# A decode attention kernel: K and V loaded in units of eight heads through a ring of three unequal regions

## The chip, the core and the metric

The kernel runs on one core of one Trainium2 chip. The metric is device time in microseconds (us) of one execution. The engines that appear below are TensorE (PE, with its weight loads shown apart as PEld), VectorE (DVE), ScalarE (ACT), GpSimd (POOL) and SyncE (SP), which issues nearly all transfers. On-chip memory is SBUF, with 128 partitions, and PSUM, which TensorE accumulates into in eight banks of 512 float32 columns per partition.

## What is computed

Two rows of `x` (batch 2, one token, 512 wide, bf16) go through two branches that a gate mixes. Cut to what matters, the reference is:

```python
g = sigmoid((x * gate_w).sum(-1, keepdims=True))
q = (x @ wq).reshape(2, 1, 32, 128)                     # 32 heads of 128
scores = einsum("bhqd,bhkd->bhqk", q, k_cache) * 128**-0.5    # k_cache: 2 x 32 x 4096 x 128
p = softmax(scores)
a = einsum("bhqk,bhkd->bhqd", p, v_cache).reshape(2, 1, 4096) @ wo
b = relu(x @ w1) @ w2                                   # 512 -> 1376 -> 512
out = g * a + (1 - g) * b
```

`k_cache` and `v_cache` are 64 MiB each; `wq` and `wo` are 4 MiB each, `w1` and `w2` 1.4 MB each. Everything is bf16. Each byte of K and V is used once.

## The kernel before

**Units and slots.** K is cut into 16 units of 4 MiB (four heads each), V likewise. Unit `u` holds 16,384 consecutive rows of 128 values, laid out so that partition `p` takes 128 consecutive rows: 32 KB per partition, one contiguous run in memory. The tile `kv` has `NSLOT` = 3 slots of 32 KB per partition; K units 0 to 15 and then V units 0 to 15 go through the slots in turn (`order`, `slot_of`, lines 188 to 199). `wreg` (32 KB per partition) is a separate tile that holds `wq`, later `w1`, later `wo`; `w2` has a tile of its own.

**Transfers.** They are all on SP's queue, in this order (lines 260 to 274): `wq`, K0 to K15, `w1` (it waits for `pe_q`, the end of the query projection, which frees `wreg`), V0 to V15, the last 96 rows of `w2`, two halves of `wo` (the first waits for `pe_h`, the end of `x @ w1`), three parts of `w2`, and the output. From the fourth unit on each transfer waits until its slot has been read: K units are read by the last of their four transposes (`kt_…`), V units by the last of their matmuls (`pe_v_…`). SP issues in order, so a transfer that waits holds back those behind it.

**K stage.** `k_turn` (line 379) is a VectorE transpose of a quarter of a unit into one of three buffers `kt` (`NKT` = 3); it sees pairs of bf16 as float32 and transposes blocks of 32 by 32. `k_scores` (lines 385 to 409) then does eight matmuls of 512 columns per turn: two weight loads, each held for four matmuls, one per PSUM bank. The weights are the queries, put into a buffer `qbuf` of zeros in such a way that a window of 128 columns places the result of each turn in its own rows of PSUM. All 64 turns accumulate in the same four banks. ScalarE copies the second batch's queries into `qbuf` as its parts come free (`q_second`).

**Softmax and spread.** `softmax` (lines 413 to 430) takes the maximum over all four banks (2,048 columns), brings it to one value per unit by two small transposes, lets ScalarE do four exponentials of 512 columns, and transposes the result back (line 427). `sm_spread` then copies the probabilities into `ptm`, block-diagonal weights whose zeros were set at the start; GpSimd, ScalarE and VectorE share this for the first group of four units, and GpSimd does the later groups.

**V stage.** `v_unit` (line 456) does 32 matmuls per unit with 16 weight columns each, four at a time on four column tiles of the array, into one PSUM bank. `v_extract` masks that bank and sums it into `X2` (lines 464 and 467); the next unit's matmuls wait for this. `x @ w1` (`ffn_h`, line 359) and its ReLU run on TensorE and VectorE after V1, the softmax denominators before V2.

**End.** `o_gather` sums `X2` into the heads' outputs, normalises and turns them into weights `oW`. `project` (line 498) multiplies them with `wo` in 32 matmuls: the first 16 wait for one half of `wo`, the others for the second. `ffn_f` (line 505) multiplies with `w2`, row group by row group, each part waiting for its own transfer, and adds the projection in between; `store` copies the result out of PSUM and the output transfer waits for both copying engines.

Order on every engine is the order in which the program lists its operations; waits are semaphores that each engine counts up.

Of the kernel before, what the change touches and what calls it, by code (L numbers as in the profile page):

```python
# [10 lines left out]
DFF = 1376  # L11
INV_SQRT_DH = 1.0 / (DH ** 0.5)

NSLOT = 3
NKT = 3

# [69 lines left out]
def bass_gated_mix__gqa_block_cached__dense_activation_relu__decode_kernel(  # L86
# [30 lines left out]
    kv = sb("kv", [128, NSLOT, 16384], dt.bfloat16)  # L117
    xTw = sb("xTw", [128, 4, 32], dt.bfloat16)
    qrow = sb("qrow", [128, 2, 4, 128], dt.bfloat16)
    wreg = sb("wreg", [128, 16384], dt.bfloat16)  # L120
    w2 = sb("w2", [128, 11, 512], dt.bfloat16)
    kt = sb("kt", [128, NKT, 2048], dt.float32)
    kt16 = kt[:, :, :].rearrange("p k n -> p (k n)").bitcast(dt.bfloat16).rearrange(
        "p (k c n two) -> p k c n two", k=NKT, c=4, two=2)
    qbuf = sb("qbuf", [128, 8, 4, 160], dt.bfloat16)
    E_sb = kt[:, 0, :].bitcast(dt.bfloat16)[:, 0:2048].rearrange("p (c n) -> p c n", c=4)
    ET_sb = kt[:, 0, :].bitcast(dt.bfloat16)[:, 2048:4096].rearrange("p (c n) -> p c n", c=4)
    ptm = sb("ptm", [128, 2, 16, 4, 2, 4, 4], dt.bfloat16)
    mpad = sb("mpad", [128, 32], dt.float32)
    mrow = sb("mrow", [128, 32], dt.float32)  # L130
    mmax = sb("mmax", [128, 16], dt.float32)
    nrow = sb("nrow", [128, 16, 2], dt.float32)
    negm = sb("negm", [128, 32], dt.float32)
    lsum = sb("lsum", [128, 4], dt.float32)
    pr_sb = sb("pr_sb", [128, 512], dt.float32)
    sel2 = sb("sel2", [128, 2], dt.float32)
    lrow = sb("lrow", [128, 1], dt.float32)
    rinv = sb("rinv", [32, 2], dt.float32)
    mask3 = sb("mask3", [128, 8, 4, 4], dt.float32)
    maskc = sb("maskc", [128, 4], dt.float32)  # L140
    selx = sb("selx", [128, 60], dt.float32)
    sell = sb("sell", [128, 2, 8, 4], dt.float32)
    s4 = sb("s4", [32, 4, 128], dt.bfloat16)
    X2 = sb("X2", [128, 2, 8, 128], dt.float32)
# [14 lines left out]
    V_B = 6  # L159
# [14 lines left out]
    names = ["x", "gw", "wq", "w1", "wo0", "wo1", "w2a", "w2b", "w2c", "w2d", "out"]  # L174
    sem = {n: nc.alloc_semaphore("sem_" + n) for n in names}
    sem_slot = [nc.alloc_semaphore(f"sem_slot{s}") for s in range(NSLOT)]
# [11 lines left out]
    order = [("k", u) for u in range(16)] + [("v", u) for u in range(16)]  # L188
    place = {what: n for n, what in enumerate(order)}

    def slot_of(what):
        return place[what] % NSLOT

    def slot_wait(what):
        return (sem_slot[slot_of(what)], 16 * (place[what] // NSLOT + 1))

    def freed(what):
        kind, u = what
        return marker(f"kt_{4 * u + 3}") if kind == "k" else marker(f"pe_v_{u}")
# [11 lines left out]
    def pe(fn, waits=(), signal=None, dwaits=()):  # L211
# [10 lines left out]
    pool(lambda g: g.memset(mask3[:], 0.0), signal="c_m3z")  # L222
    pool(lambda g: g.affine_select(out=mask3[:].rearrange("p (t f) h c -> p t f h c", t=4)[:, :, 0],
                                   in_=mask3[:].rearrange("p (t f) h c -> p t f h c", t=4)[:, :, 0],
                                   pattern=[[-32, 4], [-4, 4], [-1, 4]],
                                   compare_op=ALU.not_equal, fill=1.0, base=0, channel_multiplier=1),
         waits=["c_m3z"], signal="c_m3")
    pool(lambda g: g.memset(sell[:], 1.0), signal="c_s1")
    pool(lambda g: g.affine_select(out=sell[:], in_=sell[:], pattern=[[-16, 2], [-2, 8], [-32, 4]],
                                   compare_op=ALU.is_ge, fill=0.0, base=0, channel_multiplier=1),  # L230
         waits=["c_s1"], signal="c_s2")
    pool(lambda g: g.affine_select(out=sell[:], in_=sell[:], pattern=[[16, 2], [2, 8], [32, 4]],
                                   compare_op=ALU.is_ge, fill=0.0, base=1, channel_multiplier=-1),
         waits=["c_s2"], signal="c_sell")
    pool(lambda g: g.memset(s4[:], 0.0), signal="c_s4z")
# [4 lines left out]
    pool(lambda g: g.memset(ptm[:], 0.0), signal="c_ptm")  # L240
# [9 lines left out]
    def unit_in(what):  # L250
        kind, u = what
        rows = k_rows if kind == "k" else v_rows
        return rows[u * 16384:(u + 1) * 16384, :].rearrange("(p r) d -> p (r d)", p=128)
# [7 lines left out]
    for n, what in enumerate(order):  # L261
        waits = [freed(order[n - NSLOT])] if n >= NSLOT else []
        sp(lambda e, what=what: e.dma_start(kv[:, slot_of(what), :], unit_in(what)).then_inc(sem_slot[slot_of(what)], 16),  # L263
           waits=waits)
        if n == 15:
            sp(lambda e: e.dma_start(wreg[:, 0:5504], w1_in).then_inc(sem["w1"], 16), waits=[marker("pe_q")])
    sp(lambda e: e.dma_start(w2[0:96, 10, :], B_w2[1280:1376, :]).then_inc(sem["w2a"], 16))
    sp(lambda e: e.dma_start(wreg[:, 0:8192], wo_in[:, 0:8192]).then_inc(sem["wo0"], 16), waits=[marker("pe_h")])
    sp(lambda e: e.dma_start(wreg[:, 8192:16384], wo_in[:, 8192:16384]).then_inc(sem["wo1"], 16))
    for name, r0, r1 in (("w2b", 0, 4), ("w2c", 4, 9), ("w2d", 9, 10)):  # L270
        sp(lambda e, name=name, r0=r0, r1=r1: e.dma_start(w2[:, r0:r1, :], w2a_in[:, r0:r1, :]).then_inc(sem[name], 16))
    sp(lambda e: e.dma_start(out.rearrange("b s n -> (b s) n"), out_sb[:, :]).then_inc(sem["out"], 16),
       waits=[marker("dve_out"), marker("act_out")])
# [3 lines left out]
    def gate():  # L277
        for t in range(4):
# [19 lines left out]
        dve(lambda v: v.tensor_reduce(out=maskc[:], in_=mask3[:].rearrange("p k h c -> p c (k h)"), axis=AX.X, op=ALU.add),  # L298
            waits=["c_m3"], signal="dve_maskc")
        dve(lambda v: v.tensor_reduce(out=mrow[:, :].rearrange("p (k h) -> p k h", h=4), in_=mask3[:], axis=AX.X, op=ALU.add),  # L300
            waits=["c_m3"], signal="dve_selx0")
        dve(lambda v: v.tensor_reduce(out=selx[:, 28:32], in_=mrow[:, :].rearrange("p (k h) -> p h k", h=4), axis=AX.X, op=ALU.add),
            waits=["dve_selx0", "c_selx"], signal="dve_selx")
        dve(lambda v: v.tensor_reduce(out=sel2[:], in_=ident16[:].rearrange("p (t q) -> p q t", t=4)[:, 0:2, :], axis=AX.X, op=ALU.add),
            waits=["c_i16"], signal="dve_sel2")
        dve(lambda v: v.memset(psf(0, 128, V_B * BANK, BANK), 0.0), signal="dve_v0")

    def q_window(b, hq, u0, u1):
        halves = qT_ps.rearrange("p (s j q m) -> p s q j m", s=2, j=4, q=4)
        if u1 - u0 == 8:  # L310
            out = qbuf[32 * hq:32 * hq + 32, :, :, 32 + 32 * hq].rearrange("p (s q) j -> p s q j", s=2)
            return out, halves[32 * hq:32 * hq + 32, :, :, :, b]
        return qbuf[32 * hq:32 * hq + 32, u0, :, 32 + 32 * hq], halves[32 * hq:32 * hq + 32, u0 // 4, u0 % 4, :, b]

    def q_proj():
# [25 lines left out]
        for hq in range(4):  # L341
            out, src = q_window(0, hq, 0, 8)
            act(lambda a, out=out, src=src: a.activation(out=out, in_=src, func=ACT.Copy),
                waits=["pe_q", "c_qbuf"], signal=f"q_0_{hq}")

    def q_second(uh):
        for hq in range(4):
            out, src = q_window(1, hq, uh, uh + 1)
            act(lambda a, out=out, src=src: a.activation(out=out, in_=src, func=ACT.Copy),  # L349
                waits=[f"pe_sc_{4 * uh + 3}"], signal=f"q_1_{uh}_{hq}")  # L350

    def ffn_h():
        for ft in range(11):
            m = 128 if ft < 10 else 96
            for t in range(4):
                def fn(e, ft=ft, t=t, m=m):
                    o = t * DFF
                    cols = wreg[:, o + ft:o + 1280:10] if ft < 10 else wreg[:, o + 1280:o + 1376]
                    return e.matmul(psf(0, m, H_C0 + 2 * ft, 2), lhsT=cols, rhs=xT3[:, t, 0:2], start=(t == 0), stop=(t == 3))  # L359
                pe(fn, dwaits=([(sem["w1"], 16)] if ft == 0 and t == 0 else []),  # L360
                   signal=("pe_h" if ft == 10 and t == 3 else None))
# [11 lines left out]
    def k_turn(i):  # L373
        u, k = divmod(i, 4)
        rr, h = divmod(k, 2)
        what = ("k", u)
        pairs = kv[:, slot_of(what), :].bitcast(dt.float32).rearrange("p (r h d) -> p h r d", h=2, d=32)
        dst = kt[:, i % NKT, :].rearrange("p (r n) -> p r n", n=32)
        dve(lambda v: v.transpose(out=dst, in_=pairs[:, h, 64 * rr:64 * rr + 64, :]),  # L379
            waits=([f"pe_sc_{i - NKT}"] if i >= NKT else []), dwaits=([slot_wait(what)] if k == 0 else []), signal=f"kt_{i}")  # L380
# [8 lines left out]
    def k_scores(i):  # L389
        u, k = divmod(i, 4)  # L390
        rr, h = divmod(k, 2)
        pos = 2 * u + rr
        for two in range(2):
            for c in range(4):
                first, last = two == 0 and c == 0, two == 1 and c == 3
                waits = [f"kt_{i}"] if first else []
                if first and k == 0:
                    waits += [f"q_1_{u - 8}_{hq}" if u >= 8 else f"q_0_{hq}" for hq in range(4)]

                def fn(e, two=two, c=c):  # L400
                    out = psf(0, 128, c * BANK, 512)
                    lhsT = qbuf[:, u % 8, 2 * h + two, 32 - pos:160 - pos]
                    rhs = kt16[:, i % NKT, c, :, two]
                    start, stop = i == 0 and two == 0, i == 63 and two == 1
                    if c == 0:
                        return e.matmul(out, lhsT=lhsT, rhs=rhs, start=start, stop=stop)  # L406
                    return mm_held(e, out, lhsT, rhs, start, stop)
                pe(fn, waits=waits, signal=(f"pe_sc_{i}" if last else None))
# [178 lines left out]
```

## Time and profile before

| | us |
|---|---|
| Time, median of 3 runs (lowest to highest) | 345.83 (345.66 to 346.14) |
| The profiled execution's own time | 345.78 |
| Its span, first to last instruction | 344.5 |
| DMA rate over the span | 423 GB/s, 145.57 MB |
| VectorE busy / TensorE busy in the span | 189.6 / 201.8 |
| First transpose of K0 / of K15 starts | 22.71 / 169.97 |
| First matmul on V0 / on V15 starts | 190.09 / 329.12 |
| Last matmul ends | 342.68 |

The busy shares are averages over stages with different limits, so they are read stage by stage. The profiled execution lies 1.3 us above its span, which is time outside the instructions, and 0.05 us below the median of the runs. A view of waits says what an engine waited for; the chain of waits follows back from the last instruction to what released it.

### The profile page before, as it was taken

How to read it: one execution, taken by the hardware profiler on the slowest of the kernel's cores; microseconds unless marked ns; L12 is line 12 of the kernel's file. 1: busy time of each engine (PE TensorE's matmuls, PEld its weight loads, DVE VectorE, ACT ScalarE, POOL GpSimd, SP SyncE). 2: the span in 40 equal slices, each digit the busy share in tenths (PEclk: the TensorE clock that was granted, in tenths of full speed). 3: DMA queues.
4: the chain of work that ended last, by engine and by line, in shares of the span. 5: the costliest groups of instructions: out<-in, count | busy, mean ns of one | idle time of the engine just before them, and what ended most of it. 6: DMA issues, size and time to landing. Idle time of an engine off the chain costs nothing.

```text
span 344.5 us, 2426 instructions
## 1 busy us (share of the span) xinstructions
PE 201.8 (59%) x1240; PEld 40.6 (12%) x856; DVE 189.6 (55%) x136; ACT 15.2 (4%) x51; POOL 25.7 (7%) x32
## 2 busy tenths in 40 slices
PE   0429877878788787878790774223446443223365
PEld 0200000000000000000000241000113111000132
DVE  0848998999998999999978221111112101111121
ACT  1040000000000000000004000000000000000000
POOL 8400000000000000000001500400040000000000
PEclk9999998999999999999997565665556866555678
DMA  8999999999999999999999999999999999999995
GB/s 324 434 453 434 426 424 426 426 426 437 437 445 436 419 434 426 430 426 430 448 425 434 430 424 430 426 430 426 439 437 434 424 441 430 430 426 430 417 407 219
DMA packets 5747, 145.57 MB, mean 423 GB/s; under 512 B 645, under 2 KB 874, under 8 KB 1130
## 3 DMA queue, kind: packets, MB, share of 16 engines
q1 hardware_dynamic: 5732, 145.43, 98.5%
q8 instruction: 8, 0.13, 0.2%
q14 instruction: 1, 0.01, 0.0%
q10 hardware_dynamic: 6, 0.00, 0.0%
HBM read 145.43 MB, written 0.00 MB: 422 GB/s over the span
## 4 chain that ended last, share of the span: by engine, by line
DMA 72%; DVE 18%; PE 7%; issue 1%; SPq 1%; ACT 0%; DVEq 0%
DMA kv<-in_A_k_cache_dram 35%; DMA kv<-in_A_v_cache_dram 27%; DVE kt L379 16%; DMA wreg<-in_A_wo_dram 10%; PE PS L456 5%; PE PS L385 1%; DVE mpad L414 1%; DVE kt L427 1%; DVE ptm L440 1%; PE PS L498 1%; PE PS L406 0%; SPq L263 0%; PE PS L505 0%; DVE pr_sb L501 0%; DVE out_sb L524 0%
## 5 line engine op out<-in xcount | busy, mean ns | idle before, releaser
L379 DVE STREAM_TRANSPOSE kt<-kv 128x2048 f32<-128x2048 f32 x64 | 142.2, 2280 | 18.6 <-DMA kv<-in_A_k_cache_dram 16.6
L385 PE MATMUL PS<-kt,qbuf 128*128 128x512 bf16 x384 | 109.4, 393 | 0.0
L456 PE MATMUL PS<-kv,ptm 128*16 128x512 bf16 x512 | 56.3, 619 | 89.0 <-DMA kv<-in_A_v_cache_dram 76.7
L464 DVE TENSOR_TENSOR pr_sb<-PS,maskc 128x512 f32<-128x512 f32 x16 | 11.1, 691 | 108.6 <-PE PS L456 108.6
L406 PE MATMUL PS<-kt,qbuf 128*128 128x512 bf16 x128 | 51.1, 399 | 32.3 <-DVE kt L379 32.3
L456 PEld LDWEIGHTS PS<-kv,ptm 128*16 128x16 bf16 x512 | 16.9, 124 | 127.7 <-issue 109.3
L442 POOL COPY ptm<-kt 32x512 bf16<-32x512 bf16 x13 | 14.4, 1113 | 232.0 <-DVE lrow L428 175.2
L406 PEld LDWEIGHTS PS<-kt,qbuf 128*128 128x128 bf16 x128 | 12.5, 98 | 147.2 <-DVE kt L379 106.4
L467 DVE TENSOR_REDUCE X<-pr_sb 128x128 f32<-128x512 f32 x16 | 16.3, 1021 | 0.5
L349 ACT ACTIVATE qbuf<-PS 32x4 bf16<-32x4 bf16 x32 | 5.7, 179 | 76.5 <-PE PS L385 75.9
L527 ACT ACTIVATE out_sb<-PS 2x128 bf16<-2x128 f32 x2 | 0.5, 271 | 153.9 <-PE PS L505 153.9
L424 ACT ACTIVATE kt<-PS,negm 128x512 bf16<-128x512 f32 x4 | 2.7, 686 | 80.4 <-DVE negm L421 80.4
L279 PE MATMUL PS<-ident,x_sb 3*128 3x3 bf16 x4 | 0.3, 166 | 8.0 <-DMA x_sb<-in_gate_w_dram 8.0
L282 DVE COPY xT<-PS 128x12 bf16<-128x12 bf16 x1 | 0.2, 170 | 8.3 <-PE PS L279 8.3
L498 PE MATMUL PS<-wreg,oW 128*2 128x512 bf16 x32 | 2.9, 499 | 2.6 <-DMA wreg<-in_A_wo_dram 1.7
L220 POOL MEMSET qbuf<- 128x5120 bf16 x1 | 4.4, 4370 | 0.0
L479 PE MATMUL PS<-X,selx 128*32 128x128 f32 x32 | 4.0, 273 | 0.3 <-DVE X L467 0.3
L284 DVE COPY xTw<-xT 128x8 bf16<-128x8 bf16 x1 | 4.1, 4085 | 0.0
L365 DVE TENSOR_SCALAR hT<-PS,gm 128x10 bf16<-128x10 f32 x2 | 0.5, 228 | 6.2 <-PE PS L359 6.2
L318 PE MATMUL PS<-wreg,xTw 128*32 128x512 bf16 x32 | 3.6, 628 | 0.0
L285 DVE TENSOR_TENSOR xg<-xT 128x8 f32<-128x8 bf16 x1 | 3.6, 3630 | 0.0
L479 PEld LDWEIGHTS PS<-X,selx 128*32 128x32 f32 x32 | 3.4, 110 | 1.3 <-DVE X L467 0.6
(66 smaller groups left out, 45.8 us busy)
## 6 DMA issues: line engine op xcount, KB each, us to landing
kv<-in_A_k_cache_dram SPq DMA_DIRECT2D x16, 4096.0 KB, 20.3
kv<-in_A_v_cache_dram SPq DMA_DIRECT2D x16, 4096.0 KB, 25.4
wreg<-in_A_wq_dram SPq DMA_DIRECT2D x1, 4096.0 KB, 12.2
wreg<-in_A_wo_dram SPq DMA_DIRECT2D x2, 2048.0 KB, 32.2
wreg<-in_B_w_dram SPq DMA_DIRECT2D x1, 1376.0 KB, 23.1
w<-in_B_w_dram SPq DMA_DIRECT2D x1, 640.0 KB, 36.4
w<-in_B_w_dram SPq DMA_DIRECT2D x1, 512.0 KB, 35.3
w<-in_B_w_dram SPq DMA_DIRECT2D x1, 128.0 KB, 36.2
```

The source lines that it names most:

```text
L220: pool(lambda g: g.memset(qbuf[:], 0.0), signal="c_qbuf")
L284: dve(lambda v: v.tensor_copy(out=xTw[:, :, 0:2], in_=xT), waits=["dve_xT", "c_xTw"], signal="dve_xTw")
L349: act(lambda a, out=out, src=src: a.activation(out=out, in_=src, func=ACT.Copy), waits=[f"pe_sc_{4 * uh + 3}"], signal=f"q_1_{uh}_{hq}")
L379: dve(lambda v: v.transpose(out=dst, in_=pairs[:, h, 64 * rr:64 * rr + 64, :]), waits=([f"pe_sc_{i - NKT}"] if i >= NKT else []), dwaits=( ...
L385: return e.add_instruction(mybir.InstMatmult(start_tensor_calc=start, stop_tensor_calc=stop, tile_size=(128, 128), tile_position=(0, 0), l ...
L406: return e.matmul(out, lhsT=lhsT, rhs=rhs, start=start, stop=stop)
L442: pool(lambda e, dst=dst, src=src: e.tensor_copy(out=dst, in_=src), waits=waits, signal=f"pt{g}_{hq}")
L456: pe(lambda e, n=n, t=t, a=a, r16=r16, grp=grp, u4=u4, rows=rows: e.matmul(psf(32 * t, 32 * t + 16, V_B * BANK, 512), lhsT=ptm[:, grp % 2, ...
L464: dve(lambda e: e.tensor_tensor(out=parts, in0=psf(0, 128, V_B * BANK, 512).rearrange("p (c d) -> p c d", c=4), in1=maskc[:].unsqueeze(2). ...
L467: dve(lambda e: e.tensor_reduce(out=X2[:, b, u8, :], in_=parts.rearrange("p c d -> p d c"), axis=AX.X, op=ALU.add), waits=[f"dve_m{v}"], s ...
L479: pe(lambda e, u=u, b=b: e.matmul(psf(0, 32, O_C0, 128), lhsT=selx[:, 28 - 4 * u:60 - 4 * u], rhs=X2[:, b, u, :], start=(u == 0), stop=(u ...
L498: pe(lambda e, r=r, t=t: e.matmul(psf(32 * t, 32 * t + 2, PR_C0, 512), lhsT=oW[:, r, :], rhs=wreg[:, r * 512:(r + 1) * 512], start=(r < 4) ...
```

## The change

K and V are now cut into eight units each, of eight heads and 8 MiB: 64 KB per partition, again one contiguous run. `kv` becomes one tile of five pieces of 32 KB (`HALF` elements each) with three regions in it: A and B of 64 KB, C of 32 KB. A unit is loaded whole into A or B, or in two halves at different times (`lo` and `hi`, each the first or second 32 KB of every partition's run). Of each cache six units go whole and two in halves, so there are ten transfers for K and ten for V where there were 16 and 16. `wq` is loaded into C, `w1` into the first part of B, and at the end `wo` into C and `w2` into the upper half of B; the tiles `wreg` and `w2` are gone as tiles of their own. `w1` is loaded directly behind `wq`, ahead of K, and `ffn_h` and `ffn_relu` move ahead of the K stage. Each transfer waits for the last reader of what its region held before.

A unit has eight turns instead of four. A turn's columns now fall into two parities (`par`), because the blocks of 16 positions alternate between two heads; `k_scores` has four weight loads per turn, each held for two matmuls. The softmax has two maxima per row, one for each parity. Four exponentials remain; two transposes of twice the size follow. The spread into `ptm` is now a VectorE multiplication of the probabilities with a mask (`mask8`), once per piece, into places that rotate; no zeroing of `ptm`. V's weights have 32 columns instead of 16, a whole unit has 64 matmuls, and pieces alternate between two PSUM banks. `ptm`, `X2` and `pr_sb` lie over `kt` and `qbuf`. `wo` is cut at row group 24 instead of 16. The copies of the result count up a semaphore of their own that the output transfer waits for.

```diff
-NSLOT = 3
+HALF = 16384
+REGION = {"A": 0, "B": 2 * HALF, "C": 4 * HALF}
+WO_CUT = 24
...
-    order = [("k", u) for u in range(16)] + [("v", u) for u in range(16)]
...
+    both, lo, hi = (0, 1), (0,), (1,)
+    k_pieces = [(0, both, "A"), (1, both, "B"), (2, lo, "C"), (3, both, "A"), (4, both, "B"), (2, hi, "C"),
+                (5, both, "A"), (6, both, "B"), (7, lo, "C"), (7, hi, "A")]
+    v_pieces = [(0, both, "B"), (1, lo, "C"), (2, both, "A"), (3, both, "B"), (1, hi, "C"), (4, both, "A"),
+                (5, both, "B"), (6, lo, "C"), (7, both, "A"), (6, hi, "B")]
...
+    holder, filled = {"A": None, "B": "pe_h", "C": "pe_q"}, {"A": 0, "B": 0, "C": 0}
+    for kind, n, u, halves, region in pieces:
+        predecessor[kind, n] = holder[region]
+        filled[region] += 1
+        landed[kind, n] = (sem_region[region], 16 * filled[region])
+        holder[region] = f"{kind}_read_{n}"
...
+    def piece_in(kind, u, halves):
+        runs = (k_rows if kind == "k" else v_rows)[u * 32768:(u + 1) * 32768, :].rearrange("(p r) d -> p (r d)", p=128)
+        return runs[:, HALF * halves[0]:HALF * (halves[-1] + 1)]
...
     sp(lambda e: e.dma_start(wreg[:, :], wq_in).then_inc(sem["wq"], 16))
+    sp(lambda e: e.dma_start(w1, w1_in).then_inc(sem["w1"], 16))
+    for kind, n, u, halves, region in pieces:
+        sp(lambda e, kind=kind, u=u, halves=halves, region=region:
+           e.dma_start(piece_sb(halves, region), piece_in(kind, u, halves)).then_inc(sem_region[region], 16),
+           waits=([marker(predecessor[kind, n])] if predecessor[kind, n] else []))
+    sp(lambda e: e.dma_start(w2[0:96, 10, :], B_w2[1280:1376, :]).then_inc(sem["w2a"], 16), waits=[marker("v_read_6")])
+    sp(lambda e: e.dma_start(wreg[:, 0:512 * WO_CUT], wo_in[:, 0:512 * WO_CUT]).then_inc(sem["wo0"], 16), waits=[marker("v_read_7")])
+    sp(lambda e: e.dma_start(wreg[:, 512 * WO_CUT:HALF], wo_in[:, 512 * WO_CUT:HALF]).then_inc(sem["wo1"], 16))
...
     def k_scores(i):
...
+        for par in range(2):
+            for two in range(2):
+                for g in range(2):
...
+                        lhsT = qbuf[:, u % 4, par, 2 * h + two, 32 - pos:160 - pos]
+                        rhs = kt16[:, i % NKT, g, :, par, :, two]
...
+    def v_spread(n, n0, n1):
...
+        dve(lambda v: v.tensor_tensor(out=v_weights(n)[:, n0:n1], in0=src.unsqueeze(2).to_broadcast([128, n1 - n0, 8, 4]),
+                                      in1=mask8[:].unsqueeze(1).unsqueeze(3).to_broadcast([128, n1 - n0, 8, 4]), op=ALU.mult),
+            waits=["dve_et1", "c_mask8"] + [f"v_read_{m}" for m in prev], signal=f"pt{n}_{n0}")
...
     gate()
     q_proj()
+    ffn_h()
+    ffn_relu()
     for i in range(64):
         k_turn(i)
         if i >= 1:
             k_scores(i - 1)
     k_scores(63)
     softmax()
-    for v in range(16):
...
+    v_spread(1, 0, 32)
+    for n in range(10):
+        if n + 2 < 10:
+            v_spread(n + 2, 0, 32 * len(v_pieces[n + 2][1]))
+        v_unit(n)
+        if n == 1:
             o_denominators()
+        v_extract(n)
+        if n == 5:
             o_gather(0)
     o_gather(1)
     project()
```

## The prediction

> **What bounds the kernel now.** I read the page's slices and DMA queues first, then VectorE's timeline through the K stage, then the chain of waits at its end.
>
> ```profile
> span 344.5 us, 2426 instructions
> ...
> DMA  8999999999999999999999999999999999999995
> ...
> DMA packets 5747, 145.57 MB, mean 423 GB/s; under 512 B 645, under 2 KB 874, under 8 KB 1130
> ...
> q1 hardware_dynamic: 5732, 145.43, 98.5%
> ```
>
> SP's queue (q1) keeps all 16 DMA engines busy for 98.5% of the span: the transfers are the bound, from the first slice to the last but one. The same bytes move in both kernels, so only four things can change the time: the cost per packet, a moment when the queue is empty, the rate, and the tail behind the last transfers.
>
> ```profile
> 22.71 8.89 DVE L379 STREAM_TRANSPOSE kt<-kv 128x2048 f32<-128x2048 f32 x4 [4.72 <-DMA kv<-in_A_k_cache_dram]
> 32.49 8.89 DVE L379 STREAM_TRANSPOSE kt<-kv 128x2048 f32<-128x2048 f32 x4 [0.88 <-DMA kv<-in_A_k_cache_dram]
> 42.21 8.89 DVE L379 STREAM_TRANSPOSE kt<-kv 128x2048 f32<-128x2048 f32 x4 [0.84 <-DMA kv<-in_A_k_cache_dram]
> 53.15 8.89 DVE L379 STREAM_TRANSPOSE kt<-kv 128x2048 f32<-128x2048 f32 x4 [2.05 <-PE PS L385]
> 62.87 8.89 DVE L379 STREAM_TRANSPOSE kt<-kv 128x2048 f32<-128x2048 f32 x4 [0.83 <-DMA kv<-in_A_k_cache_dram]
> ...
> 160.25 8.89 DVE L379 STREAM_TRANSPOSE kt<-kv 128x2048 f32<-128x2048 f32 x4 [0.82 <-DMA kv<-in_A_k_cache_dram]
> 169.97 8.89 DVE L379 STREAM_TRANSPOSE kt<-kv 128x2048 f32<-128x2048 f32 x4 [0.82 <-DMA kv<-in_A_k_cache_dram]
> ```
>
> A unit lands every 9.72 us and its four transposes take 8.89: VectorE follows the transfers with 0.82 us to spare per unit. (The 2.05 us before 53.15 is put down to PE, but PE's turn 9 had long ended; K3 landed late. An instruction fetch of 16 KB on queue 8 began at 48.6 us, and one DMA engine was 1.2 us behind the others from then on.)
>
> ```profile
> 304.54 34.47 DMA wreg<-in_A_wo_dram
> 339.00 0.04 issue
> 339.05 1.90 PE PS L498 x15
> 340.95 0.02 issue
> 340.97 0.70 DVE pr_sb L501
> 341.68 0.04 issue
> 341.72 0.96 PE PS L505 x32
> ```
>
> At the end the second half of `wo` lands at 339.00, and 3.7 us of compute follow it. The last packet of `w2` ended at 341.76 in the trace's packet records, so here the computing is last, by 0.9 us.
>
> **The change, part by part.**
>
> *Packets.* The packet records (no view prints single ones) have medians of 1,214 ns for 32,768 bytes (4,224 packets: K, V, `wq`), 615 for 16,384 (`wo`), 418 for 11,008 (`w1`), 200 for 5,120, 46 for 1,024, and 9 for the 4-byte packet that counts the semaphore. They lie on one line: 15 ns plus 0.0366 ns per byte. Eight packets per engine and the semaphore give 8 x 1.214 + 0.009 = 9.72 us, the landing step above: there is no gap between queued transfers. If a row of 64 KB is one packet it should take 15 + 2,397 = 2,412 ns where two took 2,428. A whole piece saves 8 x 16 + 9 = 137 ns, and 12 whole pieces save 1.64 us. The other end, if each row goes as two packets, is the 12 semaphore packets alone: 0.11 us. A loss is not excluded, since no row here is longer than 32 KB (rival D). I take 1.64, because five sizes over a factor of 32 lie on the line.
>
> The Trainium skill, page "DMA: Bandwidth & Descriptors", section "Anatomy of one DMA", gives each transfer a fixed cost of about 2.0 us. By it 12 fewer transfers would save an estimated 24 us; the 9.72 us step leaves no room for that, and the trace decides.
>
> *Does the queue run empty?* I replay the transfers with steps of 19.31 us per whole piece, 9.72 per half and 3.35 for `w1` (8 x 0.418 + 0.009). `wq` lands at 12.98 as before (K0 at 22.69 was two steps after the start), `w1` at 16.3, K0 at 35.6, K1 at 54.9, K2's first half at 64.7, K3 at 84.0, K4 103.3, K2's second half 113.0, K5 132.3, K6 151.6, K7's halves 161.3 and 171.0. Eight transposes take 7 x 2.207 + 2.27 = 17.72 us (the x4 row is 3 x 2.207 + 2.27), so VectorE reads K0 to 53.4, K1 to 72.8, K2 first half to 81.7, K3 to 101.8, K4 to 121.1, K2 second half to 130.0, K5 to 150.1, K6 to 169.4, K7 to 187.2. The new waits on SP, each with everything behind it on hold: K1 for `pe_h`, about 23 (K0's transfer covers it to 35.6); K3 for K0's read, 53.4 against 64.7, when the queue would be empty; K4 72.8 against 84.0; K5 101.8 against 113.0; K6 121.1 against 132.3; the K7 halves 130.0 and 150.1 against 151.6 and 161.3. Then V0 goes into B and waits for K6's read: 169.4 against 171.0. This is the one tight place. The first transfer's packets began 1.0 us after its issue (0.81 to 1.81), and the semaphore is seen 0.36 us after its packet. On the engine that sets the landings: 0.36 + 0.1 to the first transpose + 17.72 + 0.02 + 1.0 = 19.2 us after K6's last packet, and K7's halves last 19.44. So it stays fed by 0.2 us. The other engines had run up to 1.7 us ahead (the semaphore's first to last count is 1.7 to 1.9 us apart from 53 us on) and would lose that lead, and a cold first packet takes 1.9 us instead of 1.2. The cost lies between 0 and 1.2 us, the second if a later instruction fetch again makes a new engine the last by what it cost at 48.6. I take 0.3, as the engine that counts has its next packet in time.
>
> *Softmax and V.* The softmax starts at 187.2 + 2.0 for PE's last turn, against 180.9 before. Maximum 2.3, four small steps 0.9, exponentials and transposes 3.4, then half of V0's spread: no row has it; 1,024 elements at L464's rate (512 in 0.69) are 1.4 us, and a quarter to three times that changes nothing. V0's matmuls run from about 197 to 205 (64 where 32 took 3.6 us). V0's reader frees B for V3, whose turn on the queue comes at 219: 14 us of cover. Later pieces have more: each takes 3.6 or 7.2 us, and in the page PE idles 76.7 us waiting for V. The spreads (up to 2.8 us each on VectorE), 32 weight columns for 16 and two banks lie in that idle time. GpSimd loses its 3.5 us of zeroing and its copies, which nothing at the end waited for.
>
> *K scores.* Four weight loads per turn instead of two.
>
> ```profile
> 174.52 0.10 PEld L406 LDWEIGHTS PS<-kt,qbuf 128*128 128x128 bf16 x1 [1.40 <-DVE kt L379]
> 174.53 0.40 PE L406 MATMUL PS<-kt,qbuf 128*128 128x512 bf16 x1 [0.22 <-DVE kt L379]
> 174.76 0.84 PE L385 MATMUL PS<-kt,qbuf 128*128 128x512 bf16 x3
> 175.22 0.10 PEld L406 LDWEIGHTS PS<-kt,qbuf 128*128 128x128 bf16 x1 [0.60 <-issue]
> 175.44 0.39 PE L406 MATMUL PS<-kt,qbuf 128*128 128x512 bf16 x1
> ```
>
> From 174.53 to 175.44 four matmuls take 0.91 us, and the next load (0.10) lies beside them. Eight take 1.82; with two more loads wholly exposed 2.02, still under VectorE's 2.21. Cost nothing, with that cover. Waits between whole pieces grow to about 1.8 us, and PE ran one turn at half speed (3.4 us) after an idle 2.38; the three `kt` buffers hold back VectorE only beyond 4.4 us.
>
> *Moved work.* `w1` is as long on the queue at 13 us as at 170. Its 44 matmuls (2.7 us) and the four ReLU steps now run before K0 lands at 35.6, on engines that wait; likewise the eight query copies for four.
>
> *Tail.* Only eight matmuls follow the last part of `wo` instead of 16: 0.95 of the 1.90 us. The first part lands 2.4 us later (7.6 after V's last piece, where the weights `oW` are ready at 7.2: 329.1 to 336.3), and its 24 matmuls end between 9.1 and 10.4, with the last part landing at 10.1. Then `w2` is next: its last packet at 341.76 and four matmuls allow PE to end at about 342.1 instead of 342.68. Bounds 0 and 0.66 us; I take 0.5.
>
> *Sum.* -1.64 + 0.3 - 0.5 = -1.84 us on the profiled execution's 345.78: 343.9. It stands 0.05 us below the median, which I leave out.
>
> **Rivals.**
>
> *B, rows of 64 KB save nothing.* 345.78 - 0.11 + 0.3 - 0.5 = 345.5. For it: packets grow from 615 to 1,214, nearly by their bytes, so little is left to save.
>
> *C, the K stage gets a pace of its own (slower).* If a turn takes p us, V0's first packet comes at 35.7 + 56p + 1.0 once p is above 2.41 (19.31/8). The queue is empty from 171.0, so the gap reaches the 2.5 us that make the total 0.7 slower at p = 2.45; at p = 2.6 it is 11 us: about 355. For it: the matmuls now read their columns in runs of 16, and PE at half clock needs 3.4 us. Against it: 1.82 now, and half clock lasted one turn (55.5 to 58.9).
>
> *D, longer rows read more slowly (slower).* Partitions are 64 KB apart in memory instead of 32, also for halves. From B's 345.5 a loss of 0.43% on the 233 us of whole pieces is enough for slower; 1% gives 347.8. Against it: `w1`'s rows 11 KB apart and `wo`'s and K's 32 KB apart lie on one line.
>
> On the same page of the Trainium skill, "Latency and other measured facts" has copies slowed by wide power-of-two row pitch, 207 GB/s against 214 at 512 KiB. An estimate by that 3.3% on K and V would be some 10 us more, and no run here has shown such a pitch.
>
> **How the numbers follow.** My forecast has 0.62 (343.0 to 344.9, with the seam's and the fetches' bounds), B 0.16, C 0.06, D 0.16. A difference of 0.2%, 0.7 us, is about what a measurement can tell. The forecast and a little of B are faster, 0.67; most of B and the mildest of D the same, 0.13; the rest slower, 0.20. The range reaches from 343.0 into D at 346.6, leaving out about 2 in 10.
>
> **What would show it.** Right: whole pieces land every 19.3 us, packets are fewer by some 1,500, VectorE's wait before V0 stays the only tight place, and few matmuls follow `wo`. Wrong: landing steps over 19.44, a DMA slice under 9 near 171 us, or transposes waiting for PE.

## The result, and the profile after

The changed kernel takes 347.24 us (median of six runs, 346.80 to 347.64) against 345.90 for the kernel before: the ratio is 1.0041, with a 95% interval of 1.003 to 1.0052. It is slower by 1.34 us where 1.84 us less was forecast, and it lies above the range, which ended at 346.6. The profiled execution took 346.80 us with a span of 345.3; it is the lowest of the six.

The page after, its slices and queue:

```profile
span 345.3 us, 2491 instructions
...
DMA  8998999989899999989989898999989899998995
...
DMA packets 4019, 145.57 MB, mean 422 GB/s; under 512 B 453, under 2 KB 682, under 8 KB 938
...
q1 hardware_dynamic: 4004, 145.43, 98.1%
```

There are 1,728 fewer packets for the same bytes: 12 x 128 of data and 12 x 16 that count semaphores. The DMA slices hold many 8s all along: a packet of 64 KB takes 2.4 us, and a slice is 8.6 us long. So they don't show by themselves whether the queue ran empty, and a slice under 9 near 171 us, which the prediction named as a sign of being wrong, settles nothing here.

VectorE's timeline through the K stage, in the same columns as before (start, length, what, idle time ahead and who ended it):

```profile
37.01 17.66 DVE L393 STREAM_TRANSPOSE kt<-kv 128x2048 f32<-128x2048 f32 x8 [14.13 <-DMA kv<-in_A_k_cache_dram]
56.43 26.43 DVE L393 STREAM_TRANSPOSE kt<-kv 128x2048 f32<-128x2048 f32 x12 [1.75 <-DMA kv<-in_A_k_cache_dram]
85.49 17.66 DVE L393 STREAM_TRANSPOSE kt<-kv 128x2048 f32<-128x2048 f32 x8 [2.62 <-DMA kv<-in_A_k_cache_dram]
104.84 26.43 DVE L393 STREAM_TRANSPOSE kt<-kv 128x2048 f32<-128x2048 f32 x12 [1.69 <-DMA kv<-in_A_k_cache_dram]
133.88 17.66 DVE L393 STREAM_TRANSPOSE kt<-kv 128x2048 f32<-128x2048 f32 x8 [2.61 <-DMA kv<-in_A_k_cache_dram]
153.24 35.20 DVE L393 STREAM_TRANSPOSE kt<-kv 128x2048 f32<-128x2048 f32 x16 [1.70 <-DMA kv<-in_A_k_cache_dram]
```

VectorE waits for transfers alone, never for TensorE: the K stage still follows the transfers. K6 lands at 153.15, and the first eight of the sixteen transposes that start at 153.24 read it. SyncE's timeline shows what that means for V0:

```profile
1.70 150.20 SPq L279 DMA_DIRECT2D kv<-in_A_k_cache_dram  x10
170.93 126.72 SPq L279 DMA_DIRECT2D kv<-in_A_v_cache_dram  x10
```

V0 is issued at 170.93. The queue holds only the rest of K7 then, which lands at 172.57. The view by stretches (length, busy time of PE, PEld, DVE, ACT and POOL with their instructions, granted clock, DMA share, GB/s) shows the hole between K and V:

```profile
150.00:168.00 18.00, 15.91 (x62) 3.05 (x30) 16.30 (x8) 0.00 (x0) 0.00 (x0) 0.91 0.98 424
168.00:172.00 4.00, 3.73 (x16) 0.68 (x7) 4.00 (x3) 0.00 (x0) 0.00 (x0) 1.00 0.74 303
172.00:176.00 4.00, 3.73 (x16) 0.68 (x7) 4.00 (x3) 0.00 (x0) 0.00 (x0) 1.00 1.16 459
176.00:196.00 20.00, 13.74 (x54) 2.52 (x26) 16.19 (x12) 2.15 (x7) 0.00 (x0) 0.96 0.97 419
```

From 168 to 172 us the DMA engines are busy for 74% of the time and move 303 GB/s. (A packet counts where it starts, which is why the next stretch has more than 1.) In the packet records, with ends matched to starts, thirteen of the sixteen engines stand still for 0.5 to 2.3 us ahead of their first packet of V0, and that packet takes 2.5 to 3.2 us where 2.42 is the rule. The other three go from K7 to V0 without a pause, and their first packet of V0 takes 3.0 to 3.2 us as well.

The end of the chain of waits after:

```profile
305.24 37.65 DMA kv<-in_B_w_dram
342.89 0.04 issue
342.93 0.58 PE PS L534 x24
343.51 0.02 issue
343.54 0.28 DVE out_sb L554
```

Before, the last half of `wo` and 3.7 us of compute ended the kernel; now it is a part of `w2`, seen at 342.89, and then its matmuls. The kernel ends almost as long after V's last piece as before: from that landing to the last matmul's end it was 342.68 - 328.99 = 13.69 us, and it is 343.51 - 329.87 = 13.64.

### The profile page after: what moved, and what is told of

Its sections match the earlier page's. It is cut to its first block, busy times and chain, and to the rows that moved or that the text cites. A ratio compares the mean times of both kernels' runs of the same rounds, so it can differ in the third digit from the quotient of the medians.

```text
span 345.3 us, 2491 instructions
## 1 busy us (share of the span) xinstructions
PE 198.2 (57%) x1230; PEld 54.0 (16%) x974; DVE 206.9 (60%) x129; ACT 14.8 (4%) x54; POOL 7.7 (2%) x20
## 4 chain that ended last, share of the span: by engine, by line
DMA 66%; DVE 19%; PE 13%; ACT 1%; issue 1%; SPq 0%; DVEq 0%
DMA kv<-in_A_k_cache_dram 28%; DMA kv<-in_A_v_cache_dram 24%; DVE kt L393 15%; DMA kv<-in_B_w_dram 11%; PE PS L482 4%; DMA kv<-in_A_wq_dram 4%; PE PS L421 3%; PE PS L400 3%; DVE kt L445 3%; PE PS L334 1%; PE PS L373 1%; DVE mpad L429 1%; DVE kt L467 1%; ACT qrow L347 0%; ACT kt L441 0%
## 5 line engine op out<-in xcount | busy, mean ns | idle before, releaser
L393 DVE STREAM_TRANSPOSE kt<-kv 128x2048 f32<-128x2048 f32 x64 | 141.1, 2273 | 24.5 <-DMA kv<-in_A_k_cache_dram 24.5
L421 PE MATMUL PS<-kt,qbuf 128*128 128x512 bf16 x256 | 106.3, 415 | 33.7 <-DVE kt L393 28.8
L400 PE MATMUL PS<-kt,qbuf 128*128 128x512 bf16 x256 | 105.7, 413 | 0.0
L482 PE MATMUL PS<-kv,kt 128*32 128x512 bf16 x512 | 46.9, 544 | 92.7 <-DMA kv<-in_A_v_cache_dram 76.7
L490 DVE TENSOR_TENSOR qbuf<-PS,maskc 128x512 f32<-128x512 f32 x10 | 6.9, 689 | 83.1 <-PE PS L482 83.0
L421 PEld LDWEIGHTS PS<-kt,qbuf 128*128 128x128 bf16 x256 | 25.6, 100 | 142.1 <-DVE kt L393 72.2
L482 PEld LDWEIGHTS PS<-kv,kt 128*32 128x32 bf16 x512 | 18.3, 129 | 120.3 <-issue 77.3
L467 DVE TENSOR_TENSOR kt<-kt,mask 128x1024 bf16<-128x1024 bf16 (+1 forms) x11 | 29.1, 2664 | 0.0
L329 ACT ACTIVATE qbuf<-PS 32x4 bf16<-32x4 bf16 (+1 forms) x40 | 7.6, 189 | 108.3 <-PE PS L400 106.9
L493 DVE TENSOR_REDUCE qbuf<-qbuf 128x128 f32<-128x512 f32 x10 | 10.2, 1019 | 0.3
L445 DVE STREAM_TRANSPOSE kt<-kt 128x1024 bf16<-128x1024 bf16 x2 | 9.3, 4825 | 1.5 <-ACT kt L441 1.5
L334 PE MATMUL PS<-kv,xTw 128*32 128x512 bf16 x32 | 3.6, 631 | 3.2 <-DMA kv<-in_A_wq_dram 3.2
```

The source lines that it names most:

```text
L329: act(lambda a: a.activation(out=out, in_=src, func=ACT.Copy), waits=waits, signal=f"q_{b}_{u}_{blk}_{par}")
L334: pe(lambda e, n=n, t=t: e.matmul(psf(32 * (n % 4), 32 * (n % 4) + 32, (QR_B + n // 4) * BANK, 512), lhsT=xTw[:, t, :], rhs=wreg[:, t * 40 ...
L393: dve(lambda v: v.transpose(out=dst, in_=pairs[:, h, 64 * a:64 * a + 64, :]), waits=([f"pe_sc_{i - NKT}"] if i >= NKT else []), dwaits=([l ...
L400: return e.add_instruction(mybir.InstMatmult(start_tensor_calc=start, stop_tensor_calc=stop, tile_size=(128, 128), tile_position=(0, 0), l ...
L445: dve(lambda v, g=g: v.transpose(out=ET_sb[:, :, 32 * g:32 * g + 32].rearrange("p w r -> p r w"), in_=E_sb[:, 32 * g:32 * g + 32, :]), wai ...
L467: dve(lambda v: v.tensor_tensor(out=v_weights(n)[:, n0:n1], in0=src.unsqueeze(2).to_broadcast([128, n1 - n0, 8, 4]), in1=mask8[:].unsqueez ...
```

## Experiments

Theory S: V0's transfer waits for the reader of K6 and the queue runs empty; the rest of the change is a small gain. Theory P, the rival: the long rows themselves lose the time, together with the instruction fetches of queue 8, beside which one 64 KB packet took 2,967 ns.

The landing steps below come from the trace's semaphore records: the time from one landing to the next, in us. Undisturbed, a whole piece takes 19.35 and a half 9.71. Each ratio is to the kernel before, measured beside the run.

| | K0 | V0 | the half behind it | piece after that | median us |
|---|---|---|---|---|---|
| changed, first profile | 20.73 | 20.12 | 10.82 | 19.35 | 347.24 |
| changed, again | 20.57 | 20.45 | 10.82 | 19.36 | 347.36 |
| seam filled | 20.88 | 19.35 | 9.71 | 9.71 (a half) | 345.19 |
| all rows 32 KB | 20.73 (9.72 + 11.01) | 20.39 (10.69 + 9.70) | 10.59 | 19.44 | 348.13 |
| K6 read late | 20.88 | 22.39 | 11.10 | 19.37 | 349.48 |
| fetch earlier | 20.76 | 20.56 | 9.72 | 19.90 | 347.31 |

**The changed kernel again.**

> The changed kernel as it is, beside the others on the same chip. Both theories: ratio to the kernel before 1.003 to 1.005. Its profile shows by how much the landing steps around V0 and the next piece (20.1 and 10.8 us in the first profile, where 19.35 and 9.71 are the steps elsewhere) move from one execution to another.

347.36 us, ratio 1.0038 (1.0025 to 1.0052). The excess sits at the same two steps behind the seam, 1.1 us in each this time.

**Seam filled.** A half of V2 goes into the upper half of region A, which K7's second half leaves free, between K7 and V0.

```diff
...
     for kind, n, u, halves, region in pieces:
+        if (kind, n) == ("v", 0):
+            sp(lambda e: e.dma_start(kv[:, HALF:2 * HALF], piece_in("v", 2, hi)).then_inc(sem["v2e"], 16), waits=[marker("k_read_6")])
+        if (kind, n) == ("v", 2):
+            halves = lo
...
-               waits=waits, dwaits=([landed["v", n]] if j == 0 else []), signal=(f"v_read_{n}" if j == nn - 1 else None))
+               waits=waits, dwaits=([landed["v", n]] + ([(sem["v2e"], 16)] if n == 2 else []) if j == 0 else []), signal=(f"v_read_{n}" if j == nn - 1 else None))
```

> The second half of V2 is loaded 9.7 us long between K7 and V0, into the upper half of region A, which K5 left long ago; V2's normal transfer then carries its first half alone. Nothing else moves. Theory S (the queue runs empty while V0 waits for K6's last transpose): V0's descriptors are queued early, its step is 19.4 us and the next half's 9.7, 0.8 and 1.1 us come back: 1.9 us less than the changed kernel, ratio to before about 0.999. Theory P (the 64 KB rows themselves, slowed by instruction fetches, lose the time): no change, ratio 1.004.

345.19 us, ratio 0.998 (0.9971 to 0.9989): 2.2 us less than the changed kernel, and less than the kernel before. Measured once more, beside its two variants at the end of this section, it was 345.24, ratio 0.9982 (0.9974 to 0.9991). Both long steps are gone, and the hole is filled. The same stretches of its profile:

```profile
168.00:172.00 4.00, 3.73 (x16) 0.68 (x7) 4.00 (x3) 0.00 (x0) 0.00 (x0) 1.00 1.09 467
172.00:176.00 4.00, 3.73 (x16) 0.68 (x7) 4.00 (x3) 0.00 (x0) 0.00 (x0) 1.00 0.91 393
```

V0's own wait is unchanged here: it is issued behind the same transpose of K6.

```profile
171.38 43.51 SPq L283 DMA_DIRECT2D kv<-in_A_v_cache_dram  x5
```

What changed is that 9.7 us of other transfer stand ahead of it. Theory P, which expected no change, is out.

**All rows 32 KB.** The changed kernel with each whole piece as two transfers.

```diff
-        filled[region] += 1
+        filled[region] += len(halves)
...
-           e.dma_start(piece_sb(halves, region), piece_in(kind, u, halves)).then_inc(sem_region[region], 16),
+           e.dma_start(piece_sb(halves, region)[:, 0:HALF], piece_in(kind, u, halves[:1])).then_inc(sem_region[region], 16),
            waits=([marker(predecessor[kind, n])] if predecessor[kind, n] else []))
+        if len(halves) == 2:
+            sp(lambda e, kind=kind, u=u, halves=halves, region=region:
+               e.dma_start(piece_sb(halves, region)[:, HALF:2 * HALF], piece_in(kind, u, halves[1:])).then_inc(sem_region[region], 16))
```

> The changed kernel's regions, order and waits, but each whole piece goes as two transfers of 32 KB per partition, so all rows are 32 KB as before. Theory S: the seam stays as it is, and a whole piece takes 19.43 us instead of 19.35: about 1.0 us more than the changed kernel, ratio 1.007. Theory P: the loss goes with the long rows: 1.3 us less, ratio 1.000.

348.13 us, ratio 1.0064 (1.0051 to 1.0076): 0.8 us more than the changed kernel, so long rows gain. The seam's loss is there with short rows too.

**K6 read late.** A reduction over 2,048 columns whose result is not used stands ahead of K6's last transpose.

```diff
+    hold = sb("hold", [128, 1], dt.float32)
...
+        if n == 7 and turn_end[n] == i:
+            dve(lambda v: v.tensor_reduce(out=hold[:], in_=ones32[:].unsqueeze(1).to_broadcast([128, 16, 128]), axis=AX.XY, op=ALU.add),
+                waits=["c_ones"])
```

> One more VectorE reduction of about 2.1 us before the last transpose of K6, so that K6 is read and V0 issued that much later. Theory S: the queue is already empty there, so every microsecond counts in full: 1.5 to 2.1 us more than the changed kernel, ratio about 1.010. Theory P: V0's issue has slack, no change.

349.48 us, ratio 1.0104 (1.009 to 1.0118): 2.1 us more than the changed kernel. Its VectorE timeline has the added operation between the transposes:

```profile
153.53 15.47 DVE L397 STREAM_TRANSPOSE kt<-kv 128x2048 f32<-128x2048 f32 x7 [1.69 <-DMA kv<-in_A_k_cache_dram]
168.93 2.24 DVE L392 TENSOR_REDUCE hold<-ones 128x1 f32<-128x2048 f32 x1
171.09 19.84 DVE L397 STREAM_TRANSPOSE kt<-kv 128x2048 f32<-128x2048 f32 x9
```

It pushes the next transpose back by 2.16 us, and all of that reaches the end (2.1 us): V0's issue has no slack left.

**The same delay in the kernel before.** V0 there takes the slot of K13, so the reduction goes ahead of K13's last transpose.

```diff
+    hold = sb("hold", [128, 1], dt.float32)
...
+        if i == 55:
+            dve(lambda v: v.tensor_reduce(out=hold[:], in_=ones32[:].unsqueeze(1).to_broadcast([128, 16, 128]), axis=AX.XY, op=ALU.add),
+                waits=["c_ones"])
```

> The kernel before, with the same VectorE reduction of 2.2 us ahead of the last transpose of K13, the unit whose slot V0 takes. Theory S: V0's transfer has K14, K15 and w1 ahead of it on the queue, some 20 us, so the delay costs nothing: ratio 1.000. If delays of VectorE in the K stage cost by themselves, up to 2.2 us, ratio 1.006.

345.71 us, ratio 0.9998 (0.9989 to 1.0007). SyncE's timeline of the kernel before, and then of this one:

```profile
159.46 19.75 SPq L263 DMA_DIRECT2D kv<-in_A_v_cache_dram  x3
```

```profile
161.76 17.87 SPq L264 DMA_DIRECT2D kv<-in_A_v_cache_dram  x3
```

V0 is issued 2.3 us later, and nothing comes of it: `w1`, the last transfer ahead of it, lands at 173.3, 11.5 us later still. A late reader costs only where its transfer is next.

**Fetch earlier.** `x @ w1` is computed twice in the beginning.

```diff
-    def ffn_h():
+    def ffn_h(done="pe_h"):
...
-                   signal=("pe_h" if ft == 10 and t == 3 else None))
+                   signal=(done if ft == 10 and t == 3 else None))
...
     gate()
     q_proj()
+    ffn_h(None)
     ffn_h()
```

> The changed kernel with x @ w1 computed twice in the beginning, while TensorE has nothing else to do: 88 more TensorE instructions ahead of the K stage, so that every later instruction fetch of queue 8 comes earlier, the one seen at 197 us at about 175 to 185, while V0 lands. If the 1.1 us in the step behind V0 come from that fetch (it holds up one DMA engine that has lost its lead at the empty queue), they move: V0's step grows from 20.1-20.5 to about 21.3, the next half's falls from 10.8 to 9.7, the time stays within 0.6 us of the changed kernel. If that step is long because the queue starts cold, it stays at 10.8.

347.31 us, ratio 1.0046 (1.0029 to 1.0063). The fetch came at 171.9 us, within the hole. The step of the half behind V0 fell from 10.82 to 9.72, so a queue that starts cold does not explain that step. V0's own step grew by little, to 20.56 where 21.3 was expected. By the packet records the fetch fell on an engine that had nothing to do: one engine stands still from 170.3 us and begins V0 at 173.20, the moment when the fetch ends. The later fetches, at 216 and 248 us, now showed instead, with V2's step at 19.90 (0.55 more) and the next half's at 10.03 (0.32 more). The time is the same: the loss moved with the fetches.

**Filled seam, rows 32 KB, and filled seam, `wo` cut at 16.** The first joins the two edits above. The second is:

```diff
-WO_CUT = 24
+WO_CUT = 16
```

> The kernel with the filled seam once more, as the one that the next two are compared with. Ratio to before 0.997 to 0.999.

> Filled seam, and all rows 32 KB (whole pieces as two transfers). What is left against the seam-filled kernel is the row length alone. From the landing steps (19.35 us against 2 x 9.715): 11 whole pieces x 0.08 = 0.9 us more, ratio about 1.0005. By the prediction's line through the packet sizes it would be 1.5 us, ratio 1.002; if long rows bring nothing, 0.1 us.

> Filled seam, with wo cut at row group 16 as before instead of 24. By the prediction's tail term 0.5 us more. By the traces 0 to 0.2: the last part of w2 is seen to land after all that waits for wo, so the matmuls behind wo are not last.

With 32 KB rows it took 345.98 us, ratio 1.0006 (0.9997 to 1.0015): the long rows are worth 0.74 us here, where eleven pieces go whole. With the cut at 16 it took 345.58, ratio 0.999 (0.9981 to 0.9999): about 0.3 us more than with the cut at 24, more than the traces had made me expect and less than the prediction had. The chains of the two show what comes last. With the cut at 24, the end is a part of `w2`; with 16, the matmuls behind `wo` are last again:

```profile
303.66 37.64 DMA kv<-in_B_w_dram
341.30 0.04 issue
341.35 0.58 PE PS L538 x24
```

```profile
302.43 35.82 DMA kv<-in_A_wo_dram
338.30 1.91 PE PS L531 x16
340.23 0.70 DVE qbuf L534
340.97 1.27 PE PS L538 x32
```

The 0.3 us are not all the cut's. In the trace with the cut at 24 TensorE's granted clock was whole when the last 24 matmuls ran, and in the one with the cut at 16 it was half (the first line below is of 24, the second of 16):

```profile
341.35 0.55 PE L538 MATMUL PS<-kv,hT 128*2 128x128 bf16 x24 [0.60 <-DMA kv<-in_B_w_dram]
341.35 0.86 PE L538 MATMUL PS<-kv,hT 128*2 128x128 bf16 x24
```

How much the cut gives by itself is not shown.

## Why the prediction was wrong

- **The empty queue, taken at 0.3 us and bounded by 1.2: this step failed.** The place was right, and so was the wait (K6's reader). The margin was right too: V0's first packets began at 171.90, 0.17 us before the last engine had ended K7, where 0.2 had been worked out. What failed is the conclusion that the loss stays small "as the engine that counts has its next packet in time". Filling the seam shows its price, 2.2 us, and it came in two parts. The first is V0's step, 0.8 to 1.1 us too long. The three engines that were fed in time still took 3.0 to 3.2 us for their first packet of V0 (2.9 to 3.4 in the second profile) and ended V0 0.6 to 0.9 us late. The working had put a slow first packet down to the other engines alone. Those restarted as slowly, and in the first profile two of them became the last ones. Why first packets are slow there is not shown; in the filled kernel none is.

  The second part is the lost lead, which the working counted only in its bound: V0's landings came together within 0.57 us where K7's had been 1.75 apart. So the fetch at 197 us found no engine far behind the others and cost 1.1 us more, which the kernel with the earlier fetch moved to other steps.

  The replay also had K6 landing at 151.6, and it came at 153.15, since the first fetch fell into K0 (20.73 instead of 19.35). That moved VectorE and the queue alike, so it changed no margin.
- **Packets, taken at 1.64 us.** Right in sign and mechanism, too large in size: the runs gave 0.74 with eleven whole pieces and 0.77 with twelve. In the records a 65,536-byte packet has a median of 2,418 ns, not 2,412, and a 32,768-byte one 1,213, so a pair saves 8 ns instead of 16. The intercept of a line through smaller packets was stretched too far.
- **Tail, taken at 0.5 us.** The matmuls behind `wo` are no longer last, as forecast, but against the kernel before that gained next to nothing: from V's last landing to the last matmul's end 13.69 us became 13.64. The bound used the end of `w2`'s last packet, 341.76, but the semaphore is seen at 342.18 in that trace. That delay had been counted at the seam and was forgotten here. The 0.3 us between the cuts at 16 and at 24 are a gain over another version of the changed kernel, not over the kernel before: with the cut at 16 the same time is 342.24 - 328.11 = 14.13 us, 0.3 of it by the half clock.
- **Rivals.** B's size for the packets was nearer than the forecast's. C named V0's wait for K6 but put it down to a K stage slowed by TensorE: VectorE waits 24.5 us in all for transfers there and for nothing else. (By C's own formula the gap of 2.5 us comes at 2.44 us a turn; at 2.45 it is 2.9.) After idle times TensorE did run at half speed, 0.43 us per matmul from 39.4 to 43.6 us, and three buffers hid it. D did not happen: neither 64 KB rows nor half rows 64 KB apart took longer per byte (2,418 and 1,213 ns). The slower copies that the Trainium skill's page "DMA: Bandwidth & Descriptors", section "Latency and other measured facts", has at wide pitch were not seen at 64 KB; the page has them from 512 KiB on, and no run here has such a pitch.
- **Softmax and spread.** Mis-sized without harm: the two transposes took 9.3 us where exponentials and transposes together were given 3.4, and the spreads 1.85 and 3.6. V0's first matmul came at 206.6 instead of 197. V3 was issued at 212.6, when V0 had been read, and the queue ahead of it ended at 222.9: 10 us of cover instead of 14 still hid it.
- **The fixed cost of a transfer.** The same page of the Trainium skill, section "Anatomy of one DMA", has about 2.0 us per transfer, as a fit to transfers that GpSimd issues; the ones here are SyncE's. Between queued transfers the trace shows none of it, as the prediction said. Where the queue was empty, filling the hole was worth 2.2 us. That the sizes agree is not shown to be more than chance, since about half of it comes with the fetch.

The three measured parts give 2.17 - 0.74 - 0.05 = 1.4 us, against 1.34 measured (1.0 to 1.8 by the interval). The filled kernel with 32 KB rows fits: without the seam and without long rows it took 345.98 against 345.80 before, so the later cut of `wo` and the moved work gain nothing that these runs can resolve.

## What to carry to other kernels

Where transfers are the bound, compare for each transfer the moment when its buffer is free with the moment when the queue ahead of it ends, less the way from issue to first packet and from last packet to semaphore (1.0 and 0.3 to 0.5 us here). Just in time was not enough here: with 0.17 us to spare the engines that were fed lost 0.6 to 0.9 us. Bigger units with the same memory shrink that cover, for V0 from some 14 us to nothing. Look for such a place at a change of stage, where the ring's order is irregular. A transfer whose buffer has long been free, put ahead of the tight one, turned a loss of 0.4% into a gain of 0.2%.

## What the runs showed of the hardware that was not expected

An instruction fetch of 16 KB on queue 8 takes 0.9 to 1.3 us, holds one DMA engine for about 1.0 us and lengthens its next packet by 0.5 (2,967 ns where 2,418 is usual). A landing counts all sixteen engines, so the first fetch shows in full (K0's or K3's step is 1.2 to 1.6 us longer in every run). It leaves the landings of the sixteen 1.7 to 2.3 us apart, and later fetches on other engines are then hidden, or cost up to 0.25 us, as long as the queue never runs empty: in the filled kernel the steps that hold the fetches at 206 and 226 us are 9.71 and 19.35. An empty queue resets this: behind it a fetch cost 1.1 us again.
